# A third PSUM bank in the rotation of the experts' first products

## The chip, the cores and the metric

One core of a Trainium2 chip runs the whole program. The metric is the device time of one execution in microseconds (us): 357.85 us before, the median of three runs (356.42 to 364.26).

## The reference

The program computes a gated linear attention and then a mixture of experts. Cut to what matters:

```python
for t in range(S):                        # 4 batches, 8 heads, 768 steps, head size 48
    state = f[:, :, t, :, None] * state + einsum('bhd,bhe->bhde', k[:, :, t], v[:, :, t])
    y[:, :, t] = einsum('bhd,bhde->bhe', q[:, :, t], state)
x = y as 3072 rows of 384
e_idx = argmax(x @ w_gate, axis=1)        # each row goes to one of 8 experts
for e in range(8):
    h  = maximum(x[mask] @ w1[e], 0.0)    # 384 -> 1024
    ye = h @ w2[e]                        # 1024 -> 384
    out[mask] = gate_w[mask, None] * eom[mask, e, None] * ye
```

All sums are kept at float32 accuracy. Each factor of a product is split into a rounded high part and the rest, and three partial products (high x high, high x rest, rest x high) are added up in PSUM.

## The kernel before

The first third of the run (to about 119 us) is the attention; it ends by scattering the rows of x to DRAM, sorted by expert. What follows are eight stages, one per expert, in the order of their sizes: `CAPS` gives the rows that a stage is built for (512, 448, 432, 416, 400, 400, 384, 376). Stages are numbered s = 0 to 7 here.

A stage has two halves on TensorE (PE). **First products**: `mm1(s, f)` for f = 0 to 7, called in `run`. One call is one group: nine matmuls (three blocks of the 384 inputs, three partial products each) add up 128 of the 1024 hidden values for all rows of the stage in one PSUM tile, `h_ps`. Then ScalarE (ACT) takes the relu of it as the high part `hh` (L852), and VectorE (DVE) reads the same tile again and subtracts `hh` for the rest `hl` (L853). Only when `hl` is written is the tile free. Stage 0 does 256 of its rows ahead of time (`mm1_early`, while the attention finishes), so its regular groups are 256 columns wide; the others are as wide as the stage's rows. **Second products**: `mm2` (L867, stages 1 to 5) or `mm2_row` (L877, stages 0, 6, 7) use `hh` and `hl` against w2 and add up in three tiles `y_ps`, all eight f into the same sums.

`h_ps` comes from the pool `mo_psh` with two buffers, each one PSUM bank. The tiles take turns, so group g may start when `hl` of group g-2 is written. The PSUM of this part of the program has eight banks: two for `h_ps`, one for transposes (`mo_psx`), three for `y_ps`, one for small results (`mo_pso`); the eighth is not used once the attention is over.

What else runs beside a stage's first products sets when DVE comes to `hl`. Every engine works its instructions off in the order of the program (`chain`, L1208, keeps that order for PE, ACT, DVE and GpSimd). Between the groups `run` puts on DVE: the low halves of the stage's w2 (`split(2, s, f // 2)` at even f, L680), steps of the gate's weight (`gain`, stages 0 and 1), and from stage 2 on the output of the stage before (`backs`: three transposes of `y_ps`, L901, and one scaling `ob`, L907). During the second products DVE and ACT prepare the next stage: its x (`x_in`, tiles `xc`, `xh`, `xl`) and its w1 (`split(1, ...)`). Loads of the weights go through SyncE's queue, rows are put out by GpSimd's indirect DMAs.

Of the kernel before, what the change touches and what calls it, by code (L numbers as in the profile page):

```python
# [8 lines left out]
F32 = mybir.dt.float32  # L9
# [7 lines left out]
PSUM = bass.MemoryType.PSUM  # L17
# [589 lines left out]
class Experts:  # L607
# [28 lines left out]
    def open_rest(self, ctx):  # L636
        pool = lambda name, bufs, **kw: ctx.enter_context(self.tc.tile_pool(name=name, bufs=bufs, **kw))
        self.wp.tile([128, 48], F32, name="w_pad", bufs=1)
        self.ha.tile([128, 16], F32, name="ha_pad", bufs=1)
        self.xp, self.hp, self.yp = pool("mo_x", 2), pool("mo_h", 9), pool("mo_y", 1)  # L640
        self.psy, self.pso = pool("mo_psy", 1, space=PSUM), pool("mo_pso", 1, space=PSUM)
        self.yps = [self.psy.tile([128, 512], F32, name=f"y_ps{d}") for d in range(KC)]


# [192 lines left out]
    def mm1(self, s, f, early=False):  # L837
        nc = self.nc
        x = "early" if early else s
        n = self.xt[x, 0][0].shape[1]  # L840
        ps = self.psh.tile([128, 512], F32, name="h_ps")
        wh, wl = self.whl[1, s, f // 2]
        i = 0
        for c in range(KC):
            cs = slice((f % 2) * 128, (f % 2) * 128 + 128)
            xh, xl = self.xt[x, c]
            for a, b in ((wh, xh), (wh, xl), (wl, xh)):
                nc.tensor.matmul(ps[:, 0:n], a[:, c, cs], b, start=(i == 0), stop=(i == 3 * KC - 1))  # L848
                i += 1
        pool, width, at = (self.ha, EARLY, 0) if early else (self.hp, WIDE, H_AT[s])  # L850
        hi, lo = (pool.tile([128, width], F32R, name=m)[:, at:at + n] for m in ("hh", "hl"))
        nc.scalar.activation(out=hi, in_=ps[:, 0:n], func=AF.Relu)  # L852
        nc.vector.scalar_tensor_tensor(out=lo, in0=ps[:, 0:n], scalar=0.0, in1=hi.bitcast(F32), op0=ALU.max,  # L853
                                       op1=ALU.subtract)
        self.hs.setdefault((s, f), []).append((hi, lo))
# [425 lines left out]
```

## Time and profile before

| | us |
|---|---|
| median of three runs | 357.85 |
| lowest and highest run | 356.42, 364.26 |
| the profiled execution, its own time | 357.65 |
| its span, first to last instruction | 355.8 |
| PE busy in the span | 343.3 (96%) |
| weight loads of PE (PEld) busy | 316.5 (89%) |
| DVE busy | 260.1 (73%) |
| ACT busy | 183.5 (52%) |

The profile is one execution; its time is 1.85 us more than its span and 0.2 us below the median. A matmul of 400 columns is listed with 0.34 us, while the next one starts 0.18 us later: matmuls overlap in the array, so that PE can read as busy although no new matmul starts. "Idle before" is the time in which an engine had nothing running ahead of an instruction, and behind the arrow stands what ended it.

### The profile page before, as it was taken

The numbers are of one execution on the slowest core, as the hardware profiler recorded it, in microseconds if no ns is written. First come the engines' busy times: TensorE is split into PE (matmuls) and PEld (weight loads), VectorE is DVE, ScalarE is ACT, GpSimd is POOL, SyncE is SP. The second block draws the span as 40 slices with busy tenths as digits, with TensorE's granted clock in tenths as the row PEclk, the third lists the DMA queues.
The fourth block names the chain that finished last, engine by engine and source line by source line (L and its number), as shares of the span: only waits on it lengthen the run. The fifth ranks groups of instructions, "written<-read, shape, count | busy, mean of one in ns | idle before, by whom it ended". The sixth has DMA issues, their size and how long they took to land. (4 is left out here: it accounts for less than half of the span.)

```text
span 355.8 us, 8327 instructions
## 1 busy us (share of the span) xinstructions
PE 343.3 (96%) x3001; PEld 316.5 (89%) x3001; DVE 260.1 (73%) x524; ACT 183.5 (52%) x437; POOL 146.6 (41%) x176
## 2 busy tenths in 40 slices
PE   8899999998999999999999999999999999999993
PEld 3788898887888899998999999999999999999993
DVE  6998989896998666675885885885975974876600
ACT  3776765775765742554632552453453453465510
POOL 7787698896988753032000005005005005007112
PEclk9999999999999999999999999999999999999999
DMA  7999999998146624989777399399599399282101
GB/s 255 350 361 355 243 219 281 229 256 249 58 134 228 246 93 150 241 221 327 178 221 129 78 335 285 53 288 313 101 322 280 64 325 287 50 282 86 38 24 44
DMA packets 81203, 73.62 MB, mean 207 GB/s; under 512 B 37058, under 2 KB 75781, under 8 KB 81152
## 3 DMA queue, kind: packets, MB, share of 16 engines
q1 hardware_dynamic: 77840, 63.35, 65.3%
q0 software_dynamic: 3312, 9.65, 7.8%
q8 instruction: 25, 0.41, 0.5%
q14 instruction: 26, 0.21, 0.2%
HBM read 57.16 MB, written 16.27 MB: 206 GB/s over the span
## 5 line engine op out<-in xcount | busy, mean ns | idle before, releaser
L927 POOL DMA_INDIRECT out<-yr,dst x20 | 21.7, 1083 | 129.1 <-DMA yr<-yd 81.5
L852 ACT ACTIVATE hh<-h_ps 128x256 fp32r<-128x256 f32 (+6 forms) x72 | 34.8, 484 | 63.6 <-PE h_ps L848 63.5
L848 PE MATMUL h_ps<-xh,w1h 128*128 128x400 f32 (+6 forms) x192 | 66.5, 346 | 1.1 <-DVE hl L853 0.8
L853 DVE SCALAR_TENSOR_TENSOR hl<-h_ps,hh 128x256 fp32r<-128x256 f32 (+6 forms) x72 | 38.8, 539 | 37.8 <-ACT hh L852 37.3
L848 PE MATMUL h_ps<-xh,w1l 128*128 128x400 f32 (+6 forms) x192 | 64.8, 337 | 0.0
L848 PE MATMUL h_ps<-xl,w1h 128*128 128x400 f32 (+6 forms) x192 | 64.7, 337 | 0.0
L867 PE MATMUL y_ps<-hh,w2h 128*128 128x400 f32 (+3 forms) x120 | 42.1, 351 | 0.0
L867 PE MATMUL y_ps<-hh,w2l 128*128 128x400 f32 (+3 forms) x120 | 42.0, 350 | 0.0
L867 PE MATMUL y_ps<-hl,w2h 128*128 128x400 f32 (+3 forms) x120 | 42.0, 350 | 0.0
L848 PEld LDWEIGHTS h_ps<-xh,w1h 128*128 128x128 f32 x192 | 36.0, 187 | 5.9 <-DVE hl L853 4.8
L848 PEld LDWEIGHTS h_ps<-xh,w1l 128*128 128x128 f32 x192 | 36.0, 188 | 0.5
L848 PEld LDWEIGHTS h_ps<-xl,w1h 128*128 128x128 f32 x192 | 36.1, 188 | 0.4
L680 DVE TENSOR_TENSOR w2l<-w2r,w2h 128x768 fp32r<-128x768 f32 x31 | 30.6, 988 | 3.1 <-ACT w2h L679 1.5
L231 POOL TENSOR_TENSOR q_t<-q_t,p 128x512 f32<-128x512 f32 x24 | 30.6, 1276 | 3.3 <-DVE p L217 2.3
L217 DVE TENSOR_TENSOR_SCAN p<-f_ps,start_p 128x511 f32<-128x511 f32 x22 | 28.0, 1275 | 4.1 <-ACT start_p L205 2.2
L347 POOL DMA_INDIRECT xs_dram<-xn,slot x24 | 24.2, 1009 | 11.3 <-DVE misc L300 4.6
L253 PE MATMUL a_ps<-q_t,k_t 64*128 64x128 f32 x384 | 27.9, 285 | 1.0 <-POOL k_t L228 0.9
L680 DVE TENSOR_TENSOR w1l<-w1r,w1h 128x768 fp32r<-128x768 f32 x28 | 26.7, 955 | 2.3 <-ACT w1h L679 1.4
L330 PE MATMUL x_ps<-turn,xt 128*128 128x112 f32 x192 | 26.3, 279 | 1.2 <-ACT xt L324 0.7
L224 DVE TENSOR_TENSOR_SCAN i<-f_ps,start_i 128x512 f32<-128x512 f32 x22 | 26.9, 1223 | 0.8
L945 POOL DMA_INDIRECT out<-o,dst x10 | 10.8, 1078 | 40.3 <-ACT o L882 21.0
L877 PE MATMUL y_ps<-w2h,hh 128*128 128x384 f32 (+1 forms) x80 | 26.9, 337 | 0.0
(182 smaller groups left out, 781.6 us busy)
## 6 DMA issues: line engine op xcount, KB each, us to landing
w1r<-in_w SPq DMA_DIRECT2D x32, 384.0 KB, 5.2
w2r<-in_w SPq DMA_DIRECT2D x32, 384.0 KB, 4.6
f_t<-in_f SPq DMA_DIRECT2D x6, 512.0 KB, 9.2
q_t<-in_q SPq DMA_DIRECT2D x6, 512.0 KB, 9.1
k_t<-in_k SPq DMA_DIRECT2D x6, 512.0 KB, 9.5
v_t<-in_v SPq DMA_DIRECT2D x6, 512.0 KB, 8.3
v_t<-in_v SPq DMA_DIRECT2D x4, 768.0 KB, 13.1
yr<-yd SPq DMA_DIRECT2D x5, 576.0 KB, 6.5
```

The lines of the kernel that those rows point to most:

```text
L217: nc.vector.tensor_tensor_scan(out=flat(d["p"])[:, 1:n], data0=flat(d["f"])[:, 0:n - 1], data1=sp[:, 1:n], initial=sp[:, 0:1], op0=ALU.mul ...
L224: nc.vector.tensor_tensor_scan(out=flat(d["i"])[:, ::-1], data0=flat(d["f"])[:, ::-1], data1=flat(k.start_i[z])[:, ::-1], initial=0.0, op0 ...
L231: nc.gpsimd.tensor_tensor(out=q_t[i][:, :, sl], in0=q_t[i][:, :, sl], in1=d["p"], op=ALU.mult)
L253: nc.tensor.matmul(aps[t][par][:, g, :], k_t[b % 2][r, g, sl], q_t[b % 2][r, g, sl], start=(g == 0), stop=(g == NP - 1))
L330: nc.tensor.matmul(xps[t][:, g, :], xt[t][:, g, :], turn[:, g, :], start=(g == 0), stop=(g == NP - 1))
L347: i = nc.gpsimd.indirect_dma_start(out=xs_dram, out_offset=bass.IndirectOffsetOnAxis(ap=r.slot[:, t:t + 1], axis=0), in_=xn[t // 4][:, t % ...
L680: (eng or self.nc.vector).tensor_tensor(out=flat(lo), in0=raw, in1=flat(hi.bitcast(F32)), op=ALU.subtract)
L848: nc.tensor.matmul(ps[:, 0:n], a[:, c, cs], b, start=(i == 0), stop=(i == 3 * KC - 1))
L852: nc.scalar.activation(out=hi, in_=ps[:, 0:n], func=AF.Relu)
L853: nc.vector.scalar_tensor_tensor(out=lo, in0=ps[:, 0:n], scalar=0.0, in1=hi.bitcast(F32), op0=ALU.max, op1=ALU.subtract)
L867: self.nc.tensor.matmul(self.yps[d][:, 0:n], a[:, d, fs], b, start=(f == 0 and i == 0), stop=(f == KF - 1 and i == 2), skip_group_check=True)
L877: self.nc.tensor.matmul(ps[0:n, 0:DM], a, b[:, f % 2, :], start=(f == 0 and i == 0), stop=(f == KF - 1 and i == 2))
```

## The change

A further pool, `mo_psh3`, is opened with one buffer, in the bank that was free. The regular groups are counted through all stages, and every third one (the count modulo 3 is 2) takes its `h_ps` from there; the others go on taking turns in the two old banks. The early groups of stage 0 keep to the two. Since two of three groups alternate between two banks, every bank is used again by the third group after: group g now waits for `hl` of group g-3.

```diff
@@ open_rest
         self.psy, self.pso = pool("mo_psy", 1, space=PSUM), pool("mo_pso", 1, space=PSUM)
+        self.psh3, self.groups = pool("mo_psh3", 1, space=PSUM), 0
         self.yps = [self.psy.tile([128, 512], F32, name=f"y_ps{d}") for d in range(KC)]
@@ mm1
-        ps = self.psh.tile([128, 512], F32, name="h_ps")
+        if early:
+            bank = self.psh
+        else:
+            bank = self.psh3 if self.groups % 3 == 2 else self.psh
+            self.groups += 1
+        ps = bank.tile([128, 512], F32, name="h_ps")
         wh, wl = self.whl[1, s, f // 2]
```

No instruction is added, taken away or put elsewhere in an engine's order; what moves are waits on PE. Two places show it. The first is PE in stage 4 (400 columns) before: the last matmul of the group f = 1, the group f = 2, and the first matmul of f = 3 (`h_ps` with its tile number, `xh` and `xl` the two parts of x, `w1h` and `w1l` those of w1).

```order
L848 MATMUL h_ps_3712<-xh2_3634,w1l_3529 128x400
L848 MATMUL h_ps_3727<-xh0_3570,w1h_3549 128x400 [waits DVE_49]
L848 MATMUL h_ps_3727<-xl0_3571,w1h_3549 128x400
L848 MATMUL h_ps_3727<-xh0_3570,w1l_3550 128x400
L848 MATMUL h_ps_3727<-xh1_3602,w1h_3549 128x400
L848 MATMUL h_ps_3727<-xl1_3603,w1h_3549 128x400
L848 MATMUL h_ps_3727<-xh1_3602,w1l_3550 128x400
L848 MATMUL h_ps_3727<-xh2_3634,w1h_3549 128x400
L848 MATMUL h_ps_3727<-xl2_3635,w1h_3549 128x400
L848 MATMUL h_ps_3727<-xh2_3634,w1l_3550 128x400
L848 MATMUL h_ps_3746<-xh0_3570,w1h_3549 128x400 [waits DVE_49]
```

The same place on PE in the changed kernel:

```order
L854 MATMUL h_ps_3715<-xh2_3637,w1l_3532 128x400
L854 MATMUL h_ps_3730<-xh0_3573,w1h_3552 128x400
L854 MATMUL h_ps_3730<-xl0_3574,w1h_3552 128x400
L854 MATMUL h_ps_3730<-xh0_3573,w1l_3553 128x400
L854 MATMUL h_ps_3730<-xh1_3605,w1h_3552 128x400
L854 MATMUL h_ps_3730<-xl1_3606,w1h_3552 128x400
L854 MATMUL h_ps_3730<-xh1_3605,w1l_3553 128x400
L854 MATMUL h_ps_3730<-xh2_3637,w1h_3552 128x400
L854 MATMUL h_ps_3730<-xl2_3638,w1h_3552 128x400
L854 MATMUL h_ps_3730<-xh2_3637,w1l_3553 128x400
L854 MATMUL h_ps_3749<-xh0_3573,w1h_3552 128x400 [waits DVE_49]
```

The wait of the group f = 2 on DVE is gone (its bank was last read in the stage before); the group f = 3 still waits on DVE, now for the `hl` of f = 0 in place of f = 1. It is so in each of the eight stages.

The second place is PE in the second products of stage 4, the nine matmuls of f = 4 and the first three of f = 5, before (`y_ps0` to `y_ps2` are the three sums, `w2h` and `w2l` the parts of w2):

```order
L867 MATMUL y_ps0_2280<-hh_3771,w2h_3775 128x400 [waits Activation_49]
L867 MATMUL y_ps0_2280<-hh_3771,w2l_3776 128x400
L867 MATMUL y_ps0_2280<-hl_3772,w2h_3775 128x400
L867 MATMUL y_ps1_2281<-hh_3771,w2h_3775 128x400
L867 MATMUL y_ps1_2281<-hh_3771,w2l_3776 128x400
L867 MATMUL y_ps1_2281<-hl_3772,w2h_3775 128x400
L867 MATMUL y_ps2_2282<-hh_3771,w2h_3775 128x400
L867 MATMUL y_ps2_2282<-hh_3771,w2l_3776 128x400
L867 MATMUL y_ps2_2282<-hl_3772,w2h_3775 128x400
L867 MATMUL y_ps0_2280<-hh_3793,w2h_3775 128x400 [waits Activation_49]
L867 MATMUL y_ps0_2280<-hh_3793,w2l_3776 128x400
L867 MATMUL y_ps0_2280<-hl_3794,w2h_3775 128x400
```

And in the changed kernel:

```order
L873 MATMUL y_ps0_2283<-hh_3774,w2h_3778 128x400 [waits Activation_49]
L873 MATMUL y_ps0_2283<-hh_3774,w2l_3779 128x400 [waits DVE_49]
L873 MATMUL y_ps0_2283<-hl_3775,w2h_3778 128x400
L873 MATMUL y_ps1_2284<-hh_3774,w2h_3778 128x400
L873 MATMUL y_ps1_2284<-hh_3774,w2l_3779 128x400
L873 MATMUL y_ps1_2284<-hl_3775,w2h_3778 128x400
L873 MATMUL y_ps2_2285<-hh_3774,w2h_3778 128x400
L873 MATMUL y_ps2_2285<-hh_3774,w2l_3779 128x400
L873 MATMUL y_ps2_2285<-hl_3775,w2h_3778 128x400
L873 MATMUL y_ps0_2283<-hh_3796,w2h_3778 128x400 [waits Activation_49]
L873 MATMUL y_ps0_2283<-hh_3796,w2l_3779 128x400
L873 MATMUL y_ps0_2283<-hl_3797,w2h_3778 128x400 [waits DVE_49]
```

Two waits on DVE stand here that were not written before, for the low half of w2 and for the `hl` of f = 5. Before, the wait of the last first-product group (f = 7, for `hl` of f = 5) had covered both already.

## Rows read from the trace of the kernel before

**Rows 1.** The page's first part: busy time, share of the span, instructions.

```profile
PE 343.3 (96%) x3001; PEld 316.5 (89%) x3001; DVE 260.1 (73%) x524; ACT 183.5 (52%) x437; POOL 146.6 (41%) x176
```

**Rows 2.** Waits from 143 us on, PE and its weight loads: us, times, longest.

```profile
PE h_ps L848 <- DVE hl L853: 0.8, 2, 0.4
...
PEld h_ps L848 <- DVE hl L853: 4.8, 12, 0.8
```

**Rows 3.** Timeline of PE, stage 5, from f = 2 to f = 3: start, duration.

```profile
277.48 0.34 PE L848 MATMUL h_ps<-xh,w1l 128*128 128x400 f32 x1
277.88 0.45 PE L848 MATMUL h_ps<-xh,w1h 128*128 128x400 f32 x1
278.17 0.34 PE L848 MATMUL h_ps<-xl,w1h 128*128 128x400 f32 x1
278.35 0.34 PE L848 MATMUL h_ps<-xh,w1l 128*128 128x400 f32 x1
```

**Rows 4.** Windows: first products of stages 0 to 7, first to next matmul's start.

```profile
143.21:152.52 9.31, 8.92 (x73) 8.55 (x73) 6.02 (x20) 4.47 (x12) 0.00 (x0) 1.00 1.04 218
160.85:175.96 15.11, 14.70 (x74) 13.44 (x74) 9.58 (x22) 7.57 (x15) 2.18 (x3) 1.00 1.01 257
190.49:204.84 14.35, 14.35 (x74) 13.29 (x73) 9.95 (x15) 6.63 (x11) 0.00 (x0) 1.00 0.60 97
218.75:232.81 14.06, 14.05 (x73) 13.22 (x73) 9.79 (x15) 6.52 (x11) 0.94 (x1) 1.00 0.62 136
246.25:259.84 13.59, 13.54 (x74) 12.80 (x73) 9.42 (x15) 6.43 (x11) 1.69 (x2) 1.00 0.72 161
272.80:286.39 13.59, 13.54 (x74) 12.80 (x73) 9.43 (x15) 6.43 (x11) 0.47 (x1) 1.00 0.56 131
299.35:312.60 13.25, 13.11 (x74) 12.39 (x74) 9.27 (x15) 6.34 (x11) 0.57 (x1) 1.00 0.50 130
325.08:337.45 12.37, 12.37 (x73) 12.30 (x73) 7.05 (x12) 7.07 (x13) 4.87 (x5) 1.00 0.16 56
```

**Rows 5.** Windows: groups without a gap, stages 0 to 6 (1, 4, then 2 each).

```profile
143.21:144.26 1.05, 1.05 (x10) 1.05 (x10) 0.15 (x1) 0.00 (x0) 0.00 (x0) 1.00 0.88 265
166.96:174.16 7.20, 7.20 (x38) 6.76 (x37) 5.99 (x13) 3.94 (x9) 0.23 (x1) 1.00 0.97 158
190.49:193.97 3.48, 3.48 (x20) 3.38 (x18) 0.86 (x2) 1.26 (x2) 0.00 (x0) 1.00 1.33 183
218.75:222.12 3.37, 3.37 (x19) 3.36 (x19) 0.80 (x2) 1.24 (x2) 0.94 (x1) 1.00 1.11 285
246.25:249.50 3.25, 3.25 (x20) 3.25 (x20) 0.74 (x2) 1.23 (x2) 1.69 (x2) 1.00 1.06 300
272.80:276.04 3.24, 3.24 (x20) 3.24 (x19) 0.74 (x2) 1.23 (x2) 0.47 (x1) 1.00 0.97 267
299.35:302.49 3.14, 3.14 (x19) 3.14 (x19) 0.67 (x2) 1.22 (x2) 0.57 (x1) 1.00 1.05 301
```

**Rows 6.** Timeline of DVE and ACT in stage 5's first products: start, duration.

```profile
276.75 0.61 DVE L901 STREAM_TRANSPOSE yt<-y_ps 128x416 f32<-128x416 f32 x1
277.29 0.54 DVE L853 SCALAR_TENSOR_TENSOR hl<-h_ps,hh 128x400 fp32r<-128x400 f32 x1
277.75 0.59 DVE L901 STREAM_TRANSPOSE yt<-y_ps 128x416 f32<-128x416 f32 x1
281.05 1.44 DVE L907 TENSOR_TENSOR ob<-yt,gain 128x1248 f32<-128x1248 f32 x1
282.41 0.56 DVE L853 SCALAR_TENSOR_TENSOR hl<-h_ps,hh 128x400 fp32r<-128x400 f32 x1
...
277.92 0.51 ACT L852 ACTIVATE hh<-h_ps 128x400 fp32r<-128x400 f32 x1 [1.18 <-PE h_ps L848]
```

**Rows 7.** Timeline of DVE: the last part of x for stage 6.

```profile
297.35 0.56 DVE L795 TENSOR_TENSOR xl<-xc,xh 128x384 fp32r<-128x384 f32 x1 [0.58 <-ACT xh L794]
```

**Rows 8.** Timeline of ACT: the program's last scaling, behind the last matmul.

```profile
350.18 0.58 ACT L882 ACTIVATE o<-y_ps,gain 120x384 f32<-120x384 f32 x1 [3.58 <-PEq L1237]
```

## The prediction

> **What bounds the kernel now.** I read four views, in this order. The page's busy times come first [rows 1]: PE is busy for 96% of the span, DVE for 73%, ACT for 52%. From 143 us on, where the changed code runs, PE is the one engine without room, so the question is only how much of its time is not matmuls. The waits are second [rows 2]: PE itself is listed as idle for 0.8 us in front of `h_ps`, its weight loads for 4.8 us in twelve places, both until DVE has written `hl`. Third, the timeline at one such place [rows 3]: in stage 5 the last matmul of f = 2 starts at 277.48 and the first of f = 3 at 277.88, 0.40 us later where 0.18 is the rule (278.17 to 278.35); the matmul after it comes at 278.17, another 0.29. So the gap costs (0.40 - 0.18) + (0.29 - 0.18) = 0.33 us, though PE reads as busy throughout. Fourth, the windows that measure all the gaps of a stage [rows 4, 5].
>
> The first two views would give different sums. [...] My own sum uses neither row, only start times.
>
> **The change, part by part.** It adds and removes no instruction, and no queue is passed. It removes one wait per stage (f = 2) and lets the others look three groups back, not two.
>
> *What the gaps cost.* I take the length of each stage's eight groups [rows 4] less eight times the period of groups without a gap [rows 5]:
>
> - stage 0: 9.31 - 8 x 1.05 = 0.91
> - stage 1: 15.11 - 8 x 7.20/4 = 0.71
> - stage 2: 14.35 - 8 x 3.48/2 = 0.43
> - stage 3: 14.06 - 8 x 3.37/2 = 0.58
> - stage 4: 13.59 - 8 x 3.25/2 = 0.59
> - stage 5: 13.59 - 8 x 3.24/2 = 0.63
> - stage 6: 13.25 - 8 x 3.14/2 = 0.69
> - stage 7: 12.37 us, or 1.55 per group of 376 columns, in line with 1.57 at 384; no gap. It has no `backs` beside it: that is the control.
>
> The sum is 4.54 us, all on PE's chain, which is without holes from one stage to the next.
>
> *How much of it goes.* In stages 2 to 6 the late `hl` have one cause: DVE works on the previous stage's output first. `hl` of f = 1 starts at 277.29 behind a transpose that began at 276.75 and ends at 277.83, and PE starts f = 3 at 277.88 [rows 3, 6]. Later the scaling of 1.44 us puts another `hl` off to 282.41 [rows 6]. With three banks a group has one whole period more, 1.05 us in stage 0 and 1.57 to 1.80 in the others. The dearest single gaps are the parts of 0.91 and 0.71 above; each stage's whole sum is smaller than the one period gained. So no wait should remain, unless lateness adds up from group to group. It does not: DVE has 9.43 us of work in 13.59 [rows 4]; without the gaps that is 9.43 of 12.96, 73%, and in stage 0 6.02 of 8.40, 72%. I take 4.5 us. From below, if only the part that PE's own row lists goes, it is 0.8 [rows 2]; from above it is 4.8 by the loads' row [rows 2].
>
> *The waits that are new in the text.* In the second products PE now waits for `w2l` at f = 4 and for `hl` at f = 5. Both are DVE work issued before the first products end, and PE comes to f = 4 only after four times nine matmuls of 0.18 us [rows 3]. I cost them at nothing; the cover is those 6.5 us. Were it gone, PE would stand for about one DVE operation per stage, 0.5 to 1.4 us [rows 6].
>
> *What is late next.* PE reaches the next stage earlier by that stage's share, so the preparation has to keep up. For stage 6 the last part of x is done at 297.35 + 0.56 = 297.91 [rows 7], while its first products start at 299.35 [rows 4]: 1.44 us to spare, against 0.63 us gained in the stage before. This work follows the `hl` on DVE, so it moves forward too. Nothing for that.
>
> *The end.* The last scaling starts behind the last matmul at 350.18 [rows 8], so the tail of scaling, scatter and landing moves with PE and keeps its length.
>
> *Opening the third pool.* Its bank was last used by the attention, which is over before stage 0, and no wait was added at its first use. Nothing.
>
> Sum: 357.65 (the profiled execution: a span of 355.8 and 1.85 around it) - 4.5 = 353.15. That execution is 0.2 us below the median of the three runs; I put the forecast at 353.2.
>
> **The rivals.**
>
> *Half of it comes back.* The third bank only postpones the wait: lateness adds up on DVE, or PE meets it at `w2l` or at the next x. For it: DVE's work in the first products comes in clusters, the scaling and a `hl` with 1.44 + 0.56 = 2.0 us in one 1.62 us period [rows 5, 6]. Against it: the 73% above. Time: 357.65 - 2.3 = 355.4. Chance 0.11.
>
> *Nothing comes.* PE already waits for something else as long, say the next stage's weights or rows, and the gaps are only where it shows. Against it: outside the first products PE has no listed wait on a load from 143 us on. Time 357.7. Chance 0.06.
>
> *Slower by three readers at once.* New is that PE can write one `h_ps` bank while ACT reads a second and DVE a third. Should matmuls slow down then, the price is per matmul: 8 x 72 = 576 first-product matmuls; at 4.5 / 576 = 8 ns each the gain is gone, and at 16 ns the time is 353.15 + 9.2 = 362.4. Against it: the state exists today with a bank of `y_ps`. From 277.92 ACT reads `h_ps`, DVE from 277.75 `y_ps`, PE writes [rows 6], and the matmuls at 278.17 and 278.35 are 0.18 apart [rows 3] as elsewhere. Chance 0.02.
>
> *Slower by the clock.* [...] Chance 0.01. [...]
>
> *The change does not act.* If two groups in a row fell on one bank, waits would grow. The order excludes it: the third of each stage's groups has lost its wait.
>
> **How the numbers follow.** The forecast case has 0.80: no rival has a row for it. The single runs of this kernel differ by 357.85 - 356.42 = 1.4 us without the highest, so the forecast's own range is 353.2 - 1.4 - 0.3 (the 4.8 bound) = 351.5 up to 354.6. To leave out no more than 2 in 10 with that spread counted, I go on to the half case and its spread: 355.4 + 1.4 = 356.8. The bound of 0.8 us gained stands at 356.9, and I end there. About 2% is what a measurement of this kernel can tell from no change, which is 7.2 us; no case of the argument gains that much, and the few per cent on either side are for the clock case, for contention at more than its 16 ns and for a median that falls on odd runs: faster 0.03, within 0.94, slower 0.03.
>
> **What would show it.** In the changed profile the wait of the `h_ps` loads for `hl` should be near nothing in place of 4.8 us; the first products of stage 5 should last 12.96 us, of stage 0 8.4, of stage 1 14.4; stage 7 should stay at 12.37. The distance from the last matmul to the end stays. The `hl` themselves stay as late on DVE as they are. Wrong would be: the same gaps at other groups (f = 4 or f = 7), a new wait of PE in front of `y_ps` or at the next stage's x, matmuls of 400 columns more than 0.18 us apart, or a granted clock below 1.00 in a stage.

## The result and the profile after

The changed kernel takes 353.36 us in the median of six runs (352.33 to 355.32), the one before 357.55 in the median of the six beside it. The ratio is 0.9877, with a 95% interval of 0.9842 to 0.9912: 1.2% faster, by clearly more than the noise and by less than 2%. One of the six runs before (364.26 us) is 2.2% above the fastest and counts as slow; without it the median is 357.24 and the fall 3.9 in place of 4.2 us. The profiled execution took 355.32 us at a span of 353.6.

The page's first part of the changed kernel answers to [rows 1]: PE has 3.5 us less of busy time, the weight loads, DVE and ACT stand about where they were.

```profile
PE 339.8 (96%) x3001; PEld 317.8 (90%) x3001; DVE 259.7 (73%) x524; ACT 183.5 (52%) x437; POOL 144.6 (41%) x176
```

The waits of the weight loads from 143 us on, where 4.8 us in twelve places stood [rows 2], come down to one row that has nothing to do with `h_ps` and stood there before too. PE itself has none.

```profile
PEld L1082 <- issue: 0.2, 1, 0.2
```

The windows of the first products, stages 0 to 7, from the first matmul's start to that of the next part, answer to [rows 4]: after the length come the busy times of PE, PEld, DVE, ACT and POOL, the granted clock, the DMA share and GB/s.

```profile
145.63:154.11 8.48, 8.48 (x73) 8.48 (x73) 5.30 (x18) 4.32 (x12) 0.00 (x0) 1.00 1.11 238
162.44:176.86 14.42, 14.42 (x73) 13.52 (x73) 9.80 (x22) 7.77 (x15) 1.54 (x3) 1.00 1.04 253
191.40:205.32 13.92, 13.92 (x74) 13.52 (x73) 9.95 (x15) 6.62 (x11) 0.00 (x0) 1.00 0.57 95
219.24:232.68 13.44, 13.44 (x73) 13.43 (x72) 9.79 (x15) 6.51 (x11) 0.94 (x1) 1.00 0.59 129
246.12:259.08 12.96, 12.96 (x73) 12.96 (x73) 9.21 (x15) 6.33 (x11) 2.06 (x3) 1.00 0.65 153
272.04:285.00 12.96, 12.96 (x73) 12.96 (x73) 9.42 (x15) 6.43 (x11) 1.86 (x2) 1.00 0.62 155
297.96:310.44 12.48, 12.48 (x73) 12.48 (x73) 9.26 (x15) 6.34 (x11) 1.11 (x2) 1.00 0.54 128
322.93:335.29 12.36, 12.36 (x74) 12.36 (x74) 7.13 (x12) 7.06 (x13) 4.87 (x5) 1.00 0.20 72
```

Read the length column: 101.02 us in sum, where the eight rows of before add up to 105.63. Stage 7 has not moved.

What DVE does has not moved either. Its timeline in stage 5 (start, duration) answers to [rows 6]:

```profile
276.00 0.61 DVE L907 STREAM_TRANSPOSE yt<-y_ps 128x416 f32<-128x416 f32 x1
276.53 0.54 DVE L859 SCALAR_TENSOR_TENSOR hl<-h_ps,hh 128x400 fp32r<-128x400 f32 x1
...
280.29 1.44 DVE L913 TENSOR_TENSOR ob<-yt,gain 128x1248 f32<-128x1248 f32 x1
281.65 0.56 DVE L859 SCALAR_TENSOR_TENSOR hl<-h_ps,hh 128x400 fp32r<-128x400 f32 x1
```

The `hl` of f = 1 begins 276.53 - 272.04 = 4.49 us into the stage, before 277.29 - 272.80 = 4.49. The one behind the scaling begins 9.61 us into it, before 9.61. The `hl` are exactly as late; only nobody waits for them.

The span fell by 2.2 us only, against 4.61 us of first products. The rest is ahead of the changed code: stage 0 begins at 145.63, before at 143.21, 2.42 us later. PE's first rows and the windows of 9.8 to 16 us show where that began:

```profile
1.26 6.57 PE L60 MATMUL kn_ps<-warm 128*128 128x512 bf16 x22 [1.26 <-DVE warm L66]
9.96 1.16 PE L253 MATMUL a_ps<-q_t,k_t 64*128 64x128 f32 x16 [2.13 <-POOL k_t L228]
```

```profile
9.80:12.00 2.20, 2.04 (x21) 1.63 (x22) 2.13 (x4) 1.80 (x6) 1.51 (x3) 0.88 1.09 352
12.00:14.00 2.00, 2.00 (x8) 0.84 (x8) 1.93 (x3) 0.93 (x3) 1.85 (x3) 0.50 1.14 329
14.00:16.00 2.00, 2.00 (x24) 1.71 (x22) 1.30 (x2) 0.67 (x2) 0.48 (x1) 0.78 1.07 357
```

In this execution PE stood idle for 2.13 us before the attention's first matmul, and the granted clock then read 0.50 from 12 to 14 us. In the profile of before it read 1.00 there. That part of the program is the same in both kernels; runs below show it with and without the fall. Behind the fall PE is 1.73 us later than before at the same matmul, the first into `two_ps` (15.80 against 14.07 us); 0.11 of it was there ahead of the fall (9.96 against 9.85), so the fall cost some 1.6 us. At the end of the attention, when PE turns the first tokens, it is 1.83 us (120.70 against 118.87). Most of the rest is one idle time of 0.56 us ahead of an early group, at 135.50, for which the profile shows no cause. So the profile understates the change, and the medians are to be read. Behind the last matmul all is as it was: the last scaling starts at 348.02, 0.43 us after the last matmul's start, and 5.6 us before the end; before that was 350.18 [rows 8] and 5.6 us.

```profile
348.02 0.58 ACT L888 ACTIVATE o<-y_ps,gain 120x384 f32<-120x384 f32 x1 [3.58 <-PEq L1243]
```

### The profile page after: what moved, and what is told of

Its sections match the earlier page's. It is cut to its first block, busy times and chain, and to the rows that moved or that the text cites. A ratio compares the mean times of both kernels' runs of the same rounds, so it can differ in the third digit from the quotient of the medians.

```text
span 353.6 us, 8327 instructions
## 1 busy us (share of the span) xinstructions
PE 339.8 (96%) x3001; PEld 317.8 (90%) x3001; DVE 259.7 (73%) x524; ACT 183.5 (52%) x437; POOL 144.6 (41%) x176
## 5 line engine op out<-in xcount | busy, mean ns | idle before, releaser
L854 PE MATMUL h_ps<-xh,w1h 128*128 128x400 f32 (+6 forms) x192 | 64.7, 337 | 0.0
L681 DVE TENSOR_TENSOR w2l<-w2r,w2h 128x768 fp32r<-128x768 f32 x31 | 31.4, 1013 | 3.3 <-ACT w2h L680 1.5
L253 PEld LDWEIGHTS a_ps<-q_t,k_t 64*128 64x128 f32 x384 | 24.0, 192 | 4.8 <-POOL k_t L228 2.6
L228 POOL TENSOR_TENSOR k_t<-k_t,i 128x512 f32<-128x512 f32 x20 | 25.6, 1279 | 3.4 <-DVE i L224 2.2
```

What stands on the lines that cost most here:

```text
L228: eng.tensor_tensor(out=k_t[i][:, :, sl], in0=k_t[i][:, :, sl], in1=d["i"], op=ALU.mult)
L253: nc.tensor.matmul(aps[t][par][:, g, :], k_t[b % 2][r, g, sl], q_t[b % 2][r, g, sl], start=(g == 0), stop=(g == NP - 1))
L681: (eng or self.nc.vector).tensor_tensor(out=flat(lo), in0=raw, in1=flat(hi.bitcast(F32)), op=ALU.subtract)
```

## The experiments

The theory: a gap is PE waiting for a bank whose `hl` DVE reaches late, the gaps are local, and one period more removes them all. The rivals: two banks are too few in any case; lateness adds up and comes back; or the gain shows elsewhere. Four kernels ran side by side first (before: 356.3 us in the median there), four others later (before: 356.04), and two got a single execution with a profile (before: 355.77).

### The changed kernel again (e0_after)

No edit.

> The changed kernel again, as the yardstick for the runs beside it on this chip. Theory (the gaps are PE waiting for a bank whose hl is late, one period of slack removes all of them): 4.5 us below the kernel before, about 353.1, and first products of 8.4, 14.4, 13.9, 13.5, 13.0, 13.0, 12.5 and 12.4 us in stages 0 to 7. Rival (part of the 4.2 us was a difference in the attention's part, since the first profile of the changed kernel reached stage 0 2.4 us later than the one before): the start of stage 0 moves by up to 2.4 us from profile to profile, while the first products stay as they are.

352.33 us, ratio 0.9877 (0.9835 to 0.9919): 4.0 us less. The first products have the lengths of the first profile to 0.01 us; stage 0 began at 144.04. The clock fell to 0.50 between 12 and 14 us here too.

### Two banks, the output steps at odd f (e1_odd_backs, e10_odd_again)

```diff
-                self.backs(1)
+                if f % 2 == 1:
+                    self.backs(1)
```

(in the loop of the first products, on the kernel before)

> Two banks as before; only the output steps of the stage before (three transposes, the scaling) are put on DVE after odd f alone, so that no period has both a w2l and a transpose. Theory (a gap is a hl that DVE reaches late behind clustered work): the gaps of stages 2 to 6, 2.92 us, go without a third bank, those of stages 0 and 1, 1.62 us, stay: about 354.7. Rival (two banks are too few whatever DVE's order is, since a hl ends some 1.5 us after its group's last matmul): the gaps stay, about 357.5. A rival on the other side: the scaling now ends after the first products, its store and fetch come later, and rows put out late hold up a stage; then above 357.5.

353.52 us, ratio 0.9914 (0.988 to 0.9948): 2.8 us less, where the theory had 2.92. That the two are so close is in part chance. By the windows of the second profile stages 2 to 6 are 3.0 us shorter in sum, which is what the theory counts; stage 7 is longer and stage 1 shorter, for reasons of their own (below). An order of DVE's work in which no period has two long items thus takes the gaps of stages 2 to 6 away without a third bank. The second profile was taken because of an oddity in the first:

> The kernel with the output steps at odd f, for a second profile. In the first one matmuls were 3% farther apart from 162 to 217 us (1.80 us per group of 432 columns where 1.74 is the rule) at a granted clock of 1.00. If that belongs to the kernel, it is there again; if it was this one execution, groups of stage 2 take 1.74 us and the first products of stages 1 to 6 14.4, 13.9, 13.4, 13.0, 13.0, 12.5 us. The late x of stage 7 (its first group 2.5 us, 0.96 too long) should be there in both.

355.58 us beside 355.77 in its one execution; it decides by its lengths alone. Windows of the second profile, first products of stages 2, 5 and 7:

```profile
189.69:203.61 13.92, 13.92 (x74) 13.51 (x72) 8.99 (x14) 6.63 (x11) 0.23 (x1) 1.00 0.65 132
270.34:283.30 12.96, 12.96 (x74) 12.96 (x73) 9.02 (x16) 6.69 (x12) 4.12 (x5) 1.00 0.87 263
321.31:335.49 14.18, 13.21 (x74) 12.22 (x73) 7.96 (x16) 7.18 (x13) 7.09 (x7) 1.00 0.22 78
```

Stages 2 and 5 have the lengths that they have with three banks, 13.92 and 12.96. Stage 7 is 1.8 us too long (0.9 in the first profile): here the order costs something. Its first group takes 2.5 us in both profiles, PE waiting for `xh` and `xl` of the new stage; in the second profile a `hl` is late as well. Why the later output steps delay that x was not followed up. The oddity (3% between 162 and 217 us) was not there again and belongs to the one execution.

Both profiles, and that of e4 below, show something else: with two banks stage 1 has no gap between f = 1 and f = 2 (1.80 us, in the profile of before 2.37). Timelines of ACT, before and then in the second profile of this kernel:

```profile
163.31 0.58 ACT L882 ACTIVATE o<-y_ps,gain 128x384 f32<-128x384 f32 x1 [3.46 <-DMA out<-o,dst]
```

```profile
162.48 0.58 ACT L882 ACTIVATE o<-y_ps,gain 128x384 f32<-128x384 f32 x1 [2.75 <-DMA out<-o,dst]
```

ACT's first `hh` of stage 1 is queued behind a scaling that waits for rows of stage 0 to land. Before, it began 163.31 - 160.85 = 2.46 us into the stage, here 162.48 - 160.72 = 1.76. How late that landing is differs from execution to execution, and so does the gap.

### The third bank in stages 0 and 1 alone (e2_third_s01)

```diff
-            bank = self.psh3 if self.groups % 3 == 2 else self.psh
+            bank = self.psh3 if self.groups % 3 == 2 and s < 2 else self.psh
```

> The third bank only in stages 0 and 1; stages 2 to 7 keep two. Theory (the gaps are local, each stage's gain adds to the others'): 1.62 us less than before, about 355.9, with first products of 8.4 and 14.4 us in stages 0 and 1 and those of stages 2 to 6 as before (14.35, 14.06, 13.59, 13.59, 13.25). Rival (what is gained early is lost again at a later wait): about 357.5 with longer stretches elsewhere.

354.85 us, ratio 0.9951 (0.9917 to 0.9985): 1.45 us less, theory 1.62. Windows of the first products of stages 0, 1 and 5:

```profile
142.69:151.17 8.48, 8.48 (x73) 8.48 (x73) 5.31 (x18) 4.33 (x12) 0.00 (x0) 1.00 1.05 236
159.50:173.92 14.42, 14.42 (x73) 13.52 (x73) 9.68 (x22) 7.81 (x15) 1.47 (x3) 1.00 1.03 259
270.80:284.39 13.59, 13.54 (x74) 12.82 (x74) 9.43 (x15) 6.43 (x11) 0.88 (x1) 1.00 0.60 143
```

Stages 0 and 1 as with the third bank everywhere, stage 5 with its old 13.59. What is gained early is not lost later: the gaps are local.

### A fourth bank (e3_four_banks)

```diff
-            bank = self.psh3 if self.groups % 3 == 2 else self.psh
+            bank = (self.psh, self.psh, self.psh3, self.psx)[self.groups % 4]
```

> A fourth bank as well, the one of the transposes, which is idle between the early part and the end: the regular groups go through four banks. Theory (with three banks no group waits any more): the same as with three, 353.1 within the noise of some 0.4%. Rival (late hl still cost something that the wait's rows do not show): below by 0.5 us or more.

351.99 us, ratio 0.9861 (0.982 to 0.9903), beside 352.33 with three: the same. Its first products last 101.03 us in all, to 0.01 us those with three banks. There was nothing left to wait for. (A second line of the edit names the tile in that bank `x_ps`; the edit of e6 below has it too.)

### One more DVE instruction per group, with two banks and with three (e4_load_two, e5_load_three)

```diff
         nc.scalar.activation(out=hi, in_=ps[:, 0:n], func=AF.Relu)
+        if s > 0:
+            nc.vector.tensor_copy(out=self.spare[:, 0:256], in_=hi.bitcast(F32)[:, 0:256])
```

(Not shown: the line that opens the tile `spare`.)

> Two banks as before, with one more DVE instruction per first-product group in stages 1 to 7: a copy of 256 columns of hh to a spare tile, ahead of hl (56 copies, some 0.2 to 0.4 us each, bounded by the 0.16 us copy of 8 columns and the 0.42 us hl of 256). Theory (with two banks a hl has 0.2 to 0.5 us to spare and every lateness beyond it is PE's): nearly all groups from f = 2 on stand, 42 groups by 0.1 to 0.4 us and the late ones by more, 6 to 15 us in all, 363 to 372. Rival (PE waits only for the clustered work): the gaps of the clusters grow by the copy, 10 places by 0.3, about 360.

> The same extra DVE copy per group with the third bank. Theory (one period of 1.55 to 1.80 us to spare swallows a copy): 0 to 1.5 us over the changed kernel, 353 to 355, with the first products of stage 7 still 12.4 us; DVE has then some 9.4 + 8 x 0.3 = 11.8 us of work in 13, so that nothing adds up. Rival (the third bank only hides the clusters of today and lateness adds up): the same cost as with two banks, 6 to 15 us, 359 to 368.

With two banks 358.95 us, ratio 1.0086 (1.005 to 1.0122): 2.9 us more. With three 352.03, ratio 0.9883 (0.9817 to 0.9948), beside 0.9877 without the copies: no cost, and the first products last 101.02 us in sum as before the copies. The first fence is DVE's row of the copies in the kernel with two banks; then come its windows, and then those of the one with three: the first products of stages 5 and 7.

```profile
L855 DVE COPY spare<-hh 128x256 f32<-128x256 f32 x56 | 15.9, 284 | 29.4 <-ACT hh L853 29.3
```

```profile
271.84:285.89 14.05, 13.70 (x73) 12.75 (x73) 10.66 (x22) 6.44 (x11) 0.88 (x1) 1.00 0.59 141
325.12:337.90 12.78, 12.78 (x73) 12.09 (x73) 8.41 (x19) 7.08 (x13) 3.79 (x4) 1.00 0.15 55
```

```profile
267.81:280.77 12.96, 12.96 (x73) 12.96 (x73) 10.59 (x22) 6.44 (x11) 1.45 (x2) 1.00 0.51 131
318.70:331.06 12.36, 12.36 (x74) 12.36 (x74) 8.37 (x19) 7.12 (x13) 4.87 (x5) 1.00 0.16 56
```

15.9 us of DVE work (the row reads the same there) cost nothing with three banks, so the cover is real and not just enough for today's clusters. With two, my size was off and the rival's nearer: stage 5 grew by 14.05 - 13.59 = 0.46 us, the gaps at f = 3 and f = 6 alone (1.84 to 2.03 and 1.79 to 2.05), and stage 7, which has no clusters, by 0.41 in small parts. I had each of 42 groups lose 0.1 us and more. Outside the clusters the copy puts `hl` off by 0.2 us only. ACT and DVE at f = 0 of stage 5, first before, then with the copy:

```profile
274.62 0.51 ACT L852 ACTIVATE hh<-h_ps 128x400 fp32r<-128x400 f32 x1 [2.71 <-PE h_ps L848]
275.16 0.57 DVE L853 SCALAR_TENSOR_TENSOR hl<-h_ps,hh 128x400 fp32r<-128x400 f32 x1 [2.55 <-ACT hh L852]
```

```profile
273.66 0.51 ACT L853 ACTIVATE hh<-h_ps 128x400 fp32r<-128x400 f32 x1 [2.73 <-PE h_ps L849]
274.40 0.57 DVE L856 SCALAR_TENSOR_TENSOR hl<-h_ps,hh 128x400 fp32r<-128x400 f32 x1
```

`hl` begins 275.16 - 275.13 = 0.03 us behind the end of `hh`, with the copy 274.40 - 274.17 = 0.23. Two banks leave 0.26 us at this width (worked out under e9), and that is enough for it.

### All regular groups in one bank (e9_one_bank)

```diff
-            bank = self.psh3 if self.groups % 3 == 2 else self.psh
+            bank = self.psh3
```

> All regular groups in one bank, the new one. Theory (a group may start when the hl of the group that used its bank before is written; that hl ends 1.5 us after the last matmul's start where DVE is free, 0.5 us and more later where it is not): each of 56 groups stands for about 1.5 us or more, 85 to 110 us over the kernel with three banks, 440 to 465. Rival (PE also waits for something besides the bank, so that lengths do not follow from when hl ends): clearly outside of that.

434.27 us, 82 us over three banks, a little under the 85 that I had as the lower end. PE's timeline in stage 4, from the last matmul of f = 0 to the first of f = 1:

```profile
284.47 0.34 PE L854 MATMUL h_ps<-xh,w1l 128*128 128x400 f32 x1
286.01 0.45 PE L854 MATMUL h_ps<-xh,w1h 128*128 128x400 f32 x1 [1.20 <-DVE hl L859]
```

The emptying of a bank takes 286.01 - 284.47 = 1.54 us from the last matmul's start, 1.36 more than the usual 0.18. With the 0.11 us that the second matmul behind a wait comes late, this is 1.47, and 82 / 56 = 1.46 us per group fits. With two banks a group of the other bank lies in between, which gives 1.62 + 0.18 = 1.80 us at 400 columns: 0.26 us to spare where DVE comes at once, and that is why the gaps of stages 2 to 6 were small and in the clusters.

Stage 0, with 256 columns, has nothing to spare. The kernel before, from the last matmul of f = 0 to the first of f = 2:

```profile
144.15 0.28 PE L848 MATMUL h_ps<-xh,w1l 128*128 128x256 f32 x1
144.88 0.42 DVE L853 SCALAR_TENSOR_TENSOR hl<-h_ps,hh 128x256 fp32r<-128x256 f32 x1 [1.52 <-ACT hh L852]
145.36 0.38 PE L848 MATMUL h_ps<-xh,w1h 128*128 128x256 f32 x1
```

DVE stood ready, and still PE came 145.36 - 144.15 = 1.21 us behind the last matmul, where a period and the usual distance make 1.06 + 0.12 = 1.18. So in stage 0 the rival that two banks are too few in any case holds, for about 0.3 of its 0.83 us (the groups f = 1 to 4 take 1.10 to 1.15 us each in place of 1.06); the larger part is one `hl` behind a `w1l`.

### The early groups too (e6_early_third)

```diff
         if early:
-            bank = self.psh
+            bank = self.psx if f % 3 == 2 else self.psh
```

> The changed kernel, and the eight early groups of stage 0 go through three banks too (every third one takes the bank of the transposes, which is free at that time). Theory (the early groups have gaps of the same kind: 0.1 us and more at f = 3, 5 and 7, and 0.7 us between f = 1 and f = 2): 0.5 to 1.0 us less than the changed kernel beside it (352.3 on this chip), about 351.6. Rival (the early groups wait for the routing's small matmuls and for w1l, and PE waits later for x anyway): no change.

351.63 us, ratio 0.987 (0.9821 to 0.9919), against 0.9877 without: no difference that can be measured. The early groups are 0.56 us shorter (9.85 us from the first matmul's start to the last's, 10.41 in e0_after), but then, in this profile, PE waits at the transposes of the other tokens. Its waits between 118 and 146 us:

```profile
PE x_ps L789 <- DMA first_x<-xs_dram: 0.9, 1, 0.9
```

In e0_after that wait is not listed. It looks like the rival, but the load of these rows was slow in this execution. Its row between 134 and 146 us (the last figure is the time from issue to landing), first in e0_after, then here:

```profile
first_x<-xs_dram SPq DMA_DIRECT2D x1, 401.0 KB, 3.4
```

```profile
first_x<-xs_dram SPq DMA_DIRECT2D x1, 401.0 KB, 4.5
```

In the seven other profiles that record this landing it took 3.1 to 3.4 us. PE was ready for the rows 3.6 us after their issue here, so with the usual time it would not have waited, and in e0_after it came 1.3 us after the landing, more than the 0.56 gained. Whether the 0.56 us are waited away or kept is open: the medians do not resolve so little.

### More warm-up at the start (e7_warm27)

```diff
-WARM = 22
+WARM = 27
```

> The changed kernel with 27 in place of 22 warm-up matmuls at the very start. In three profiles the granted clock read 0.50 from 12 to 14 us, where PE had stood for some 2 us between the last warm-up matmul (7.8 us) and the first of the attention (10.0); in three others the warm-up matmuls lasted to 8.95 and the clock stayed at 1.00. Theory (the idle time brings the clock down, and five matmuls of 0.21 us bridge half of it): the fall goes, 1 to 2 us less where it happened, 350.5 to 352. Rival (the warm-up then delays the attention's first matmul, or the clock falls all the same): no change or up to 1 us more.

352.14 us, ratio 0.989 (0.9841 to 0.9938): no gain. PE's first rows:

```profile
1.26 7.74 PE L60 MATMUL kn_ps<-warm 128*128 128x512 bf16 x27 [1.26 <-DVE warm L66]
9.63 1.16 PE L253 MATMUL a_ps<-q_t,k_t 64*128 64x128 f32 x16 [0.63 <-POOL k_t L228]
```

The idle time is 0.63 us, and the granted clock read 1.00 throughout in this profile. But stage 0 began at 142.84, inside the 140.96 to 145.63 of kernels with 22 warm-up matmuls: what the attention takes varies by more than the fall costs (the profiles without the fall alone have 140.96 to 144.09). No kernel here was faster than the changed one by more than the noise.

## Why the prediction was right, point by point

**The bound.** PE's chain set the time, and what was taken out of it came off the total. The span shows it to within 0.1 us: 2.42 later into stage 0, 4.61 less in the first products, -2.2 in all.

**The sum of the gaps.** In us, forecast and found (before less after, by the windows):

| stage | 0 | 1 | 2 | 3 | 4 | 5 | 6 | 7 | sum |
|---|---|---|---|---|---|---|---|---|---|
| forecast | 0.91 | 0.71 | 0.43 | 0.58 | 0.59 | 0.63 | 0.69 | 0 | 4.54 |
| found | 0.83 | 0.69 | 0.43 | 0.62 | 0.63 | 0.63 | 0.77 | 0.01 | 4.61 |

The two terms that are off by 0.08 come from the base: stage 0's was read as 1.05 where its groups run at 1.06, stage 6's as 1.57 where they run at 1.56. Start times gave all this. The 0.8 us of PE's own idle row would have been wrong by a factor of almost six, while the 4.8 us of waits of the loads came close. The busy shares do not show the gain: that of the matmuls reads 96% before and after, that of the loads 89% and 90%.

The cause that the prediction gave is for stages 2 to 6, and e1 bears it out there. For stages 0 and 1 it gave a sum without a cause; the runs show two banks that are a little short and a `w1l` on DVE in stage 0, and a late `hh` of ACT in stage 1.

**Where it holds less.** The medians fell by 4.2 (3.9 without the run of 364.26) and 4.0 us, not 4.54. The 0.71 of stage 1 belonged in part to the execution that I read: three profiles with two banks do not have that gap, and without it the sum is 3.83. The measured values lie between. The step that was too certain is that one execution stands for all. That the forecast of 353.2 us meets the median of 353.36 so closely is in part luck: single runs of the changed kernel spread over 3 us.

**That no wait remains.** All 56 boundaries between regular groups of a stage are without a wait in the changed profile, a fourth bank adds nothing, and 15.9 us of further DVE work adds nothing. DVE's 73% was the right argument against lateness that adds up.

**Costed at nothing.** The waits written anew in front of `y_ps` never stood: the second products last 13.92, 13.44 and 12.96 us (behind stages 2, 3 and 4), before 13.91, 13.44 and 12.96. The x of the next stage came in time in every stage. The tail kept its length, 5.6 us.

**The rivals.** Three readers at once: matmuls of 400 columns stay 0.18 us apart (12.96 / 72); excluded. The granted clock in the first products: 1.00 in all eight windows, and in every window of them from the experiments above; that a stage's first products fall to a lower clock, and what that would cost, no window shows. Half or nothing comes back: e2 and e5 speak against both, in this place; for the early groups e6 leaves it open.

## What to carry to other kernels

Where a tuned engine reads as busy all through, take start-to-start times, and compare each group with the fastest of its kind: small gaps that repeat are worth their sum (here 4.61 us), and a control stage without the suspected neighbour tells whose they are (here stage 7, 12.37 and 12.36 us). A further buffer pays the lateness, as far as its one period covers it (here a stage's gaps came to 0.83 us at most, where the period is 1.06); a better order of the other engine's work can pay much of the same (here the 3.0 us of stages 2 to 6, less what stage 7 lost) where no buffer is to be had. How many buffers are enough can be read off: the time from a group's last matmul to the next write of its bank, against the periods of the groups in between (here 1.54 us, against 1.80 with one group of 400 columns in between). And a new wait behind a removed gap is no proof that the gain was waited away: look first whether what it waits for came as fast as in other profiles (here 4.5 us, in e0_after 3.4).

## What the runs showed of the hardware that was not expected

The granted clock fell to 0.50 for some 3 us between 10 and 15 us in three profiles (the changed kernel, e0_after, e3_four_banks), in which PE had stood idle for 2.13, 1.98 and 2.18 us before the attention's first matmul. It stayed at 1.00 in the profile of before (0.91), e2 (0.91), e5 (1.83) and e6 (1.11), but in the second profile of the odd-f kernel also after 2.19 us. So a longer idle time goes with it and does not decide alone. Nor does the record of the granted clock show all: it reads 1.00 from 0 to 9.8 us in all eleven profiles that were read there, though the first warm-up matmuls (6 to 13 of them) begin 0.427 us apart and the others 0.216. The earlier this distance halves, the earlier the warm-up ends, and with it the idle time begins. When it ended does separate the profiles: at 7.47, 7.69 and 7.83 us in the three with the fall, at 7.88 (e5) to 9.05 in the eight without. With so small a margin between them this shows no cause.

In the first profile of e1_odd_backs, from 162 to 217 us, matmuls of 432 columns were 0.200 us apart in place of 0.193, with a granted clock of 1.00 in all windows and no wait listed; the second profile did not have it. What slowed PE by 3% without showing in the granted clock stays open.
